# Threshold attention and SwiGLU feed-forward: 48 block loads of q and k move from SyncE's queue to GpSimd's own, the last group's output copies get buffers of their own, and the planner's ranks are set anew

## The chip, the cores and the metric

The kernel runs on one core of one Trainium2 chip. The metric is device time in microseconds (us) of one execution; the time before is the median of three runs. A profile of one execution, taken by the hardware profiler, goes with it. Its span, 532.7 us, is a little shorter than the device time of that run, 534.45 us. Five engines work beside each other: TensorE (PE in the profile, with its weight loads as PEld), VectorE (DVE), ScalarE (ACT), GpSimd (POOL) and SyncE (SP), the last used here only to issue DMAs. A queue name with a q (SPq, POOLq, ACTq) is an engine's instruction queue.

## What is computed

```python
batch, n_heads, seq, head_dim = (8, 8, 576, 64)        # q, k, v
scores = scale * np.matmul(q, k.transpose(0, 1, 3, 2))
thresh = np.max(scores, axis=-1, keepdims=True) - tau
scores = np.where(scores >= thresh, scores, -1000000000.0)
attn = softmax(scores)                                  # written out in the reference
attn_out = np.matmul(attn, v)
x = attn_out.transpose(0, 2, 1, 3).reshape(4608, 512)
xn = x / sqrt(mean(x * x) + 1e-6) * rms_g
g, val = xn @ w_gate, xn @ w_val                        # 512 -> 1536
out = (silu(g) * val) @ w_out                           # 1536 -> 512, float32
```

Only scores within `tau` (0.02) of the row's largest are kept, the rest is masked away before the softmax.

## The kernel before

**The work.** A batch has 576 rows: 512 "main" rows, cut into four chunks of 128, and 64 "tail" rows; the tails of two batches make one virtual chunk. That gives 36 chunks. A step is one chunk and one pair of heads, so there are 144 steps. One step runs so: TensorE writes the scores of two heads to PSUM (L697), VectorE copies them to a score buffer `ssb` with a running minimum of the negated scores (L730), GpSimd adds tau (`nth`, L771), ScalarE masks with a steep Prelu (L782, one per head) and takes the exponential to fp16 `wsb` (L789), a DMA transpose issued by SyncE turns it (`wt`, L849; the first 16 steps use TensorE instead), and every second step TensorE multiplies with v (L870, L875) and VectorE divides by the sums (L892, L893). After the four pairs of a chunk the rows are normalised (ScalarE L910, GpSimd L913 to L918), turned by one more DMA transpose (`xnT`, L922) and joined to groups of two or four chunks for the feed-forward part: gate and value matmuls (L976, L981), tanh on ScalarE (L990), two VectorE operations (L993, L998), the output matmuls (L1047, or L1022 in the last group), a copy out of PSUM that multiplies with 0.5 (L1060 on VectorE or L1062 on ScalarE) and a store (L1069, L1072, L1077). The feed-forward part of earlier chunks fills TensorE between the score bursts of later ones. At the end, from about 467 us on, only feed-forward work is left.

**Inputs.** Batches 0 and 1 take q and k through TensorE transposes. From batch 2 on (`BLOCKED = 2`) a batch's q and k come as 8 block loads, 288 KB each, 128 rows of 2304 contiguous bytes (`emit_block_loads`, L376): two pairs of heads for k, two for q, and the same again for the other half. So six batches make 48 loads, all issued by SyncE. They land in `qkx`. GpSimd then swaps 32x32 blocks in place through `spare` (L390, 24 copies a batch), and VectorE's 32x32 transposes (L403, L408, L412) turn the blocks into `qkt`, where the score matmuls read them. The buffer of a block is free again when VectorE's transposes of the batch before have read it. v is loaded by SyncE too (L609, L623) and rounded to fp16 by GpSimd (L584). The output weights are the only loads that GpSimd issues in the kernel before (L1138, four of 384 KB).

**Who sets the order.** Nothing is scheduled by hand line by line: `add` records each operation with an engine, a cost in ns, a priority (about the step it belongs to) and what it depends on. `order_ops` then plays a list scheduler: each engine takes, of those operations that could start first, the one with the lowest priority number, after `RANK` has been added to it by engine and kind. Loads marked `bulk` also hold back while more than 3.5 us of planned transfers are outstanding, and `gated` ties a load to the score burst of a given step. The result is a fixed sequence for each engine, and each engine runs its sequence in order: an instruction that waits holds up everything behind it on that engine. `LAT_QB` is the planned latency of a block load.

**The end.** The last group is "streamed": its four output tiles are accumulated in the four banks of the score tiles, and the last 4 of 12 slices of each tile are done tile after tile, in the order j = 0, 1, 2, 3. Tiles 0 and 2 are copied by VectorE, 1 and 3 by ScalarE. Tiles 0 and 1 go to the two output buffers `osb[0]`, `osb[1]`, which the group before has used as well, tiles 2 and 3 to score buffers, which are free by then. Each tile leaves in two stores of 64 rows.

## Time and profile before

| | before |
|---|---|
| device time, median of 3 runs | 534.09 us (533.53 to 534.13) |
| span of the profile | 532.7 us |
| mean granted TensorE clock | 0.999 |
| score bursts | from about 7 us to 467 us |
| feed-forward only | about 467 us to 527 us |
| GpSimd copies of L390, one | 0.66 us, 144 of them |
| DMA transposes of L849, issue on SyncE's queue | 1.32 us median, 128 of them |

The page of the profile gives, for each engine, the time in which it was busy, then the chain of work that ended last, followed back from the end, and the groups of instructions. A line of a group names the source line, the engine, the operation, what is written and what is read, shapes, and a count, then busy time, mean length and the idle time ahead. The timeline is in order of time: start, length (from the first start to the last end where several are merged), engine, line, operation, tiles, count, and in brackets the engine's idle time before it with what is thought to have ended it. That last part is inferred: a wait for several things is put down to the one that seems to have come last, and where a DMA was the last this can be wrong. In the table of waits each line is total us, number of times and the longest.

### The profile page before, as it was taken

Reading aid. Unit: us, or ns where it says so; the run is one execution under the profiler, and the core shown is the slowest. Engines: PE = TensorE matmul, PEld = TensorE weight load, DVE = VectorE, ACT = ScalarE, POOL = GpSimd, SP = SyncE. Lnnn points to the kernel's source line nnn. Section 1 sums busy time; section 2 is a strip of 40 time slices with the busy share of each in tenths; the row PEclk is TensorE's granted clock in tenths of the full one; section 3 lists DMA queues with packets and bytes.
Section 4 is the critical chain, followed back from the end, with each engine's and each line's share of the span. In section 5 each row is a group of like instructions: output and inputs, shape, how many; then the busy total and the mean of one; then the engine's idle time right before and its main releaser. Section 6 shows DMA issues by size and latency. Waiting matters only on the chain.

```text
span 532.7 us, 14403 instructions
## 1 busy us (share of the span) xinstructions
PE 521.8 (98%) x5368; PEld 275.2 (52%) x5368; DVE 465.3 (87%) x1347; ACT 444.0 (83%) x648; POOL 223.9 (42%) x478
## 2 busy tenths in 40 slices
PE   8999999999999999999999999999999999999995
PEld 4666676654555454545454544454545454454442
DVE  4899999979999899989997999999999898865641
ACT  5999999989997899889987998889998999952210
POOL 2368777424762165627733165626652111111000
PEclk9999999999999999999999999999999999999999
DMA  9999989979987888999989698998897677652003
GB/s 198 244 295 281 234 157 178 177 150 236 173 169 159 176 164 178 167 193 210 170 166 180 151 168 174 191 219 167 171 204 135 111 124 128 135 110 65 19 22 98
DMA packets 218886, 88.51 MB, mean 166 GB/s; under 512 B 195264, under 2 KB 204992, under 8 KB 218816
## 3 DMA queue, kind: packets, MB, share of 16 engines
q1 hardware_dynamic: 216016, 85.49, 80.9%
q0 software_dynamic: 1600, 1.57, 1.8%
q8 instruction: 42, 0.69, 0.5%
q10 hardware_dynamic: 1200, 0.52, 0.4%
q14 instruction: 28, 0.23, 0.1%
HBM read 37.75 MB, written 9.44 MB: 89 GB/s over the span
## 4 chain that ended last, share of the span: by engine, by line
PE 68%; DVE 12%; ACT 8%; DMA 4%; issue 3%; POOL 2%; SPq 1%; DVEq 0%; POOLq 0%; ACTq 0%
PE s_ps L697 21%; PE ring L1047 12%; PE ring L981 12%; PE ring L976 12%; DVE ssb L730 7%; ACT ssb L782 4%; PE ring L875 4%; DMA wt<-wsb 2%; PE s_ps L1022 2%; ACT wsb L789 2%; DMA qkx<-in_q_dram 2%; DVE sl L993 1%; PE ring L870 1%; ACT th L990 1%; PE s_ps L1047 1%
## 5 line engine op out<-in xcount | busy, mean ns | idle before, releaser
L782 ACT ACTIVATE ssb<-ssb,nth 128x576 f32<-128x576 f32 x288 | 209.2, 766 | 21.3 <-POOL nth L771 20.7
L730 DVE CUSTOM_DVE_ANT_0 ssb<-s_ps,zcol 128x576 f32<-128x576 f32 (+8 forms) x288 | 169.4, 634 | 6.2 <-PE s_ps L697 5.5
L697 PE MATMUL s_ps<-qkt 64*64 64x288 f32 (+8 forms) x2256 | 171.2, 411 | 1.2 <-DVE mx L730 0.8
L789 ACT ACTIVATE wsb<-ssb 128x1152 f16<-128x1152 f32 x144 | 166.7, 1158 | 2.2
L697 PEld LDWEIGHTS s_ps<-qkt 64*64 64x64 f32 x2256 | 81.9, 134 | 66.6 <-issue 28.0
L976 PE MATMUL ring<-xnT,wg 128*128 128x512 f16 (+1 forms) x464 | 109.2, 358 | 0.6 <-DVE sl L993 0.5
L981 PE MATMUL ring<-xnT,wv 128*128 128x512 f16 (+1 forms) x456 | 106.9, 357 | 0.5 <-DVE sl L993 0.2
L990 ACT ACTIVATE th<-ring 128x512 f32<-128x512 f32 (+1 forms) x116 | 62.5, 541 | 39.6 <-PE ring L976 39.2
L771 POOL TENSOR_SCALAR nth<-mx 128x2 f32<-128x2 f32 x144 | 30.8, 214 | 149.4 <-DVE mx L730 140.6
L993 DVE SCALAR_TENSOR_TENSOR sl<-th,ring 128x512 f32<-128x512 f32 (+1 forms) x116 | 71.9, 622 | 11.5 <-ACT th L990 11.2
L981 PEld LDWEIGHTS <-wv 128*128 128x128 f16 x480 | 44.6, 98 | 50.1 <-issue 10.8
L976 PEld LDWEIGHTS <-wg 128*128 128x128 f16 x480 | 43.0, 98 | 52.6 <-issue 15.1
L730 DVE CUSTOM_DVE_ANT_0 ssb<-s_ps,zcol,mxp 128x128 f32<-128x128 f32 (+7 forms) x112 | 52.8, 508 | 13.5 <-PE s_ps L697 13.3
L875 PE MATMUL ring<-va,wt 128*128 128x65 f16 (+1 forms) x1280 | 51.1, 193 | 0.0
L875 PEld LDWEIGHTS <-wt 128*128 128x128 f16 (+1 forms) x1280 | 46.1, 100 | 5.0 <-issue 0.6
L1047 PE MATMUL ring<-wo,hf 128*128 128x512 f16 x204 | 47.7, 379 | 0.0
L998 DVE TENSOR_TENSOR stg<-ring,sl 128x512 f16<-128x512 f32 (+1 forms) x57 | 35.5, 627 | 2.4
L998 DVE TENSOR_TENSOR hf<-ring,sl 128x512 f16<-128x512 f32 (+1 forms) x57 | 35.4, 626 | 1.8
L1047 PE MATMUL ring<-wo,stg 128*128 128x512 f16 x156 | 36.5, 379 | 0.0
L390 POOL COPY spare<-qkx 32x576 f32<-32x576 f32 x48 | 31.6, 658 | 8.7 <-DMA qkx<-in_k_dram 3.5
L893 DVE TENSOR_TENSOR xsb<-ring,rz 128x256 f32<-128x256 f32 x72 | 30.5, 424 | 3.5
L1047 PEld LDWEIGHTS <-hf 128*128 128x128 f16 x216 | 20.0, 98 | 25.8 <-issue 3.5
(75 smaller groups left out, 482.7 us busy)
## 6 DMA issues: line engine op xcount, KB each, us to landing
vst<-in_v_dram SPq DMA_DIRECT2D x32, 256.0 KB, 4.1
qkx<-in_k_dram SPq DMA_DIRECT2D x24, 288.0 KB, 3.5
qkx<-in_q_dram SPq DMA_DIRECT2D x24, 288.0 KB, 3.4
out_dram<-osb SPq DMA_DIRECT2D x51, 128.0 KB, 2.6
stg<-in_moe_w_gate_dram SPq DMA_DIRECT2D x6, 512.0 KB, 6.5
stg<-in_moe_w_val_dram SPq DMA_DIRECT2D x6, 512.0 KB, 6.4
wt<-wsb SPq DMA_TRANSPOSE x128, 3.6
out_dram<-osb SPq DMA_DIRECT2D x8, 256.0 KB, 3.0
```

The costliest lines, as they stand in the source:

```text
L390: nc.gpsimd.tensor_copy(out=dst, in_=at)
L697: nc.tensor.matmul(s_ps[h][rows, at:at + hi - lo], lhs(hs), k_of(bb, p, h)[hs, lo:hi], start=True, stop=True)
L730: nc.vector.tensor_tensor_reduce(out=ssb_of(s)[:, h, lo:hi], in0=s_ps[h][:, at:at + hi - lo], in1=zcol.to_broadcast([128, hi - lo]), scale ...
L782: nc.scalar.activation(out=sb_[:, h], in_=sb_[:, h], func=PRELU, scale=-1.0, bias=nth[m][:, h:h + 1], **PRELU_KW)
L789: nc.scalar.activation(out=wsb[s % NW], in_=sb_, func=AF.Exp)
L875: nc.tensor.matmul(ring[o.slot[0]][rs, at:at + D + 1], w[:, 5 * h + j, rs], va[vi][:, p, 2 * j + h], start=False, stop=(h == 1 and j == 3))
L976: nc.tensor.matmul(ring[o.slot[0]][:, 0:n], wg[d][:, fs], xnT[slot][:, d, 0:n], start=(d == 0), stop=(d == 3))
L981: nc.tensor.matmul(ring[o.slot[0]][:, 0:n], wv[d][:, fs], xnT[slot][:, d, 0:n], start=(d == 0), stop=(d == 3))
L990: nc.scalar.activation(out=th[i][:, 0:n], in_=ring[g.slot[0]][:, 0:n], func=AF.Tanh, scale=0.5)
L993: nc.vector.scalar_tensor_tensor(out=sl[i][:, 0:n], in0=th[i][:, 0:n], scalar=1.0, in1=ring[g.slot[0]][:, 0:n], op0=ALU.add, op1=ALU.mult)
L998: nc.vector.tensor_tensor(out=hf[hi][:, 0:n], in0=ring[vv.slot[0]][:, 0:n], in1=sl[i][:, 0:n], op=ALU.mult)
L1047: nc.tensor.matmul(ring[(first or o).slot[0]], hf[hs[fc][0]][:, 128 * j:128 * (j + 1)], wo[:, fc], start=(fc == 0), stop=(fc == NFC - 1))
```

## The change

Four edits. First, the 48 block loads of q and k are issued by GpSimd, and the planner is told so, with 880 ns of GpSimd's time each and a latency of 5.0 us in place of 4.0. Second, all four output tiles of the last group get parts of the score buffers, so that none of them shares a buffer with the group before. Third, the very last tile is copied in two halves of 256 columns, one by VectorE and one by ScalarE. Fourth, the planner's ranks are changed; kinds without an entry have rank 0. The first is for SyncE's queue, which carries all transposes, loads and stores in one order; the second and third are for the end; the fourth sets the order anew around the other three.

```diff
 RANK = dict(
-    ACT={"emit_ffn/ev": 450, "emit_ffn/store": 110, "emit_ffn/tanh": -300, "emit_k_tail/ev": -210, "emit_q_tail/ev": -80, "emit_qk/ev": 370,
-        "emit_softmax/ex2": 60, "emit_softmax/prelu": 220, "emit_x/sq": -330},
-    DVE={"emit_blocks/turn_k": 120, "emit_blocks/turn_kt": 288, "emit_blocks/turn_q": 293, "emit_burst/ttr": -57.4, "emit_ffn/ev": 320,
-        "emit_ffn/gate": 60, "emit_ffn/silu": -59, "emit_k_tail/ev": 80, "emit_qk/ev": -20, "emit_softmax/ev": 320, "emit_x/ev": 50},
-    PE={"emit_av/fn": -370, "emit_burst/fn": 16, "emit_ffn/gmm": 20, "emit_ffn/omm": 23, "emit_ffn/vmm": -40, "emit_k_tail/tr": 210, "emit_q_tail/tr":
-        -160, "emit_qk/tr": 60, "emit_softmax/tr": -40, "emit_x/trp": 20},
-    POOL={"emit_block_loads/swap": 40, "emit_softmax/nthr": -240, "emit_x/mean": -150, "emit_x/norm": -10, "round_/<lambda>": 130, "main/<lambda>":
-        700, "main/cast": -280},
+    ACT={"emit_ffn/ev": 440, "emit_ffn/store": 100, "emit_ffn/tanh": -280, "emit_k_tail/ev": -210, "emit_q_tail/ev": -60, "emit_qk/ev": 360,
+        "emit_softmax/ex2": 70, "emit_softmax/prelu": 250, "emit_x/sq": -300},
+    DVE={"emit_av/half": 10, "emit_blocks/turn_k": 120, "emit_blocks/turn_kt": 270, "emit_blocks/turn_q": 300, "emit_burst/ttr": -50,
+        "emit_ffn/ev_half": 20, "emit_ffn/silu": -47, "emit_k_tail/ev": 70, "emit_softmax/ev": 360, "emit_x/ev": 80},
+    PE={"emit_av/fn": -380, "emit_ffn/gmm": 20, "emit_ffn/omm": 22.5, "emit_ffn/vmm": -20, "emit_k_tail/tr": 220, "emit_q_tail/tr": -170,
+        "emit_qk/tr": 60, "emit_softmax/tr": -20, "emit_x/trp": 27.5},
+    POOL={"emit_block_loads/load": 10, "emit_block_loads/swap": 50, "emit_softmax/nthr": -250, "emit_x/mean": -140, "emit_x/norm": -20,
+        "round_/<lambda>": 120, "main/cast": -210},
 )
...
-    osb += [ssb[0][:, 0, 0:DM], ssb[0][:, 0, 0:DM], ssb[1][:, 0, 0:DM], ssb[2][:, 0, 0:DM]]
+    osb += [ssb[i % 3][:, i // 3, 0:DM] for i in range(4)]
...
-                    nc.sync.dma_start(out=own[:, a].rearrange("p r d -> p (r d)"),
+                    nc.gpsimd.dma_start(out=own[:, a].rearrange("p r d -> p (r d)"),
...
-                los.append(gated(add("SP", COST["sp_qb"], pr, before, load, dma=DMA_NS["qkb"] / GROUP, bulk=True), pr))
+                los.append(gated(add("POOL", COST["pool_dma"], pr, before, load, dma=DMA_NS["qkb"] / GROUP, bulk=True), pr))
...
-            oi = 2 + j if streamed and j > 1 else count["o"] % 2
+            oi = 2 + j if streamed else count["o"] % 2
...
+            final = streamed and j == len(parts) - 1
+
-            def ev(o, oi=oi, mo=mo, at=at, on_dve=on_dve):
+            def ev(o, oi=oi, mo=mo, at=at, on_dve=on_dve, cols=slice(DM // 2 if final else 0, DM)):
                 if on_dve:
-                    nc.vector.tensor_scalar(out=osb[oi], in0=ring[mo.slot[at]], scalar1=0.5, scalar2=None, op0=ALU.mult)
+                    nc.vector.tensor_scalar(out=osb[oi][:, cols], in0=ring[mo.slot[at]][:, cols], scalar1=0.5, scalar2=None, op0=ALU.mult)
                 else:
-                    nc.scalar.activation(out=osb[oi], in_=ring[mo.slot[at]], func=AF.Copy, scale=0.5)
+                    nc.scalar.activation(out=osb[oi][:, cols], in_=ring[mo.slot[at]][:, cols], func=AF.Copy, scale=0.5)
+
+            def ev_half(o, oi=oi, mo=mo, at=at):
+                cols = slice(0, DM // 2)
+                nc.vector.tensor_scalar(out=osb[oi][:, cols], in0=ring[mo.slot[at]][:, cols], scalar1=0.5, scalar2=None, op0=ALU.mult)
...
+            e = [e] + ([add("DVE", 340.0, pr - PUSH[0], [last_out[j]], ev_half)] if final else [])
...
-LAT_QB = 4000.0
+LAT_QB = 5000.0
```

More of the change, by code (lines that the diff above doesn't have):

```diff
@@ L1081, in emit_ffn @@
                     frees=(mo, at))
+            e = [e] + ([add("DVE", 340.0, pr - PUSH[0], [last_out[j]], ev_half)] if final else [])
             late = late and kind == "m"
-            osb_use[oi] = add("ACT" if late else "SP", (1100.0 if b >= BLOCKED else COST["sp"]) if kind == "m" else 1100.0, pr, [e], store,
+            osb_use[oi] = add("ACT" if late else "SP", (1100.0 if b >= BLOCKED else COST["sp"]) if kind == "m" else 1100.0, pr, e, store,
                               dma=DMA_NS['out'])
```

## The prediction

> **What bounds the kernel now.** I read the page first, engines and chain; then the table of waits; then the block loads in the list of DMA issues and on SyncE's queue; last the timeline of the end. Busy time by engine, and the chain by engine:
>
> ```profile
> PE 521.8 (98%) x5368; PEld 275.2 (52%) x5368; DVE 465.3 (87%) x1347; ACT 444.0 (83%) x648; POOL 223.9 (42%) x478
> PE 68%; DVE 12%; ACT 8%; DMA 4%; issue 3%; POOL 2%; SPq 1%; DVEq 0%; POOLq 0%; ACTq 0%
> ```
>
> TensorE is the bound: in nearly every 10 us stretch after 50 us it is busy 9.5 to 10 of 10, and the change gives it no matmul more or less. A gain can only come from a wait of TensorE that goes away, or from the few us after its last matmul. From 470 to 527 us nothing but feed-forward matmuls is left, 48 per 10 us, back to back.
>
> The table of waits says how much of TensorE's time hangs on the things that are moved:
>
> ```profile
> PE ring L870 <- DMA wt<-wsb: 1.0, 2, 0.8
> PEld L870 <- DMA wt<-wsb: 1.2, 2, 0.9
> ACT ssb L782 <- POOL nth L771: 20.7, 28, 2.2
> POOL spare L390 <- DMA qkx<-in_k_dram: 3.5, 3, 1.5
> ```
>
> TensorE waits 1.0 + 1.2 = 2.2 us in all for transposed weights that come through SyncE's queue. No engine but GpSimd waits for a block load, 3.5 us in three places, before swaps; VectorE's turns (L403, L408, L412) follow with no idle time ahead of them in any instance. So the loads are hidden now. The chain does give "DMA qkx<-in_q_dram" 1.7%, 3.89 us of it from 125.72 to 129.61. But the next link is ScalarE's Prelu at 129.63, which reads no q: it follows `nth`, which ran on GpSimd from 129.38 for 0.21 us. The load merely landed at the same moment, and I count that share as nothing.
>
> What one issue costs, on SyncE and on GpSimd (the second fence is the one line that GpSimd issues now, durations min/median/max in ns):
>
> ```profile
> qkx<-in_k_dram SPq DMA_DIRECT2D x24, 288.0 KB, 3.5
> qkx<-in_q_dram SPq DMA_DIRECT2D x24, 288.0 KB, 3.4
> wo<-in_moe_w_out_dram POOLq DMA_DIRECT2D x4, 384.0 KB, 7.9
> ```
>
> ```profile
> L1138 POOL DMA_DIRECT2D wo<-in_moe_w_out_dram x4: 828/857/990, 40.9 to 58.6; - x4
> ```
>
> SyncE's queue where loads and transposes meet:
>
> ```profile
> 121.82 0.45 SPq L376 DMA_DIRECT2D qkx<-in_q_dram  x1
> 122.38 3.29 SPq L849 DMA_TRANSPOSE wt<-wsb  x2
> 125.72 0.57 SPq L376 DMA_DIRECT2D qkx<-in_q_dram  x1
> 126.46 3.88 SPq L849 DMA_TRANSPOSE wt<-wsb  x2
> ```
>
> A load takes about 0.57 us of the queue, and here a transpose starts right after it, so it may have been held up by it. In the queue's timeline I count 13 of the 48 loads that have a transpose within 0.2 us behind them.
>
> The end:
>
> ```profile
> 522.77 0.69 DVE L1060 TENSOR_SCALAR osb<-ring 128x512 f32<-128x512 f32 x1 [4.79 <-PE ring L1047]
> 523.49 1.10 SPq L1077 DMA_DIRECT2D out_dram<-osb  x2
> 524.50 0.69 DVE L1060 TENSOR_SCALAR osb<-s_ps 128x512 f32<-128x512 f32 x1 [1.03 <-PE s_ps L1022]
> 526.30 0.69 DVE L1060 TENSOR_SCALAR ssb<-s_ps 128x512 f32<-128x512 f32 x1 [1.11 <-PE s_ps L1022]
> 527.02 1.10 SPq L1069 DMA_DIRECT2D out_dram<-ssb  x2
> 527.16 0.60 ACT L1062 ACTIVATE osb<-s_ps 128x512 f32<-128x512 f32 x1 [10.71 <-PE s_ps L1022]
> 527.66 0.59 ACT L1062 ACTIVATE ssb<-s_ps 128x512 f32<-128x512 f32 x1
> 528.86 0.59 SPq L1069 DMA_DIRECT2D out_dram<-ssb  x1
> ```
>
> Tile 2's copy starts at 526.30, so tile 1, which is done before it, was ready by about 525.4. Its copy (ScalarE, `osb`) starts only at 527.16. The line blames TensorE; I read it as the buffer: `osb[1]` was last stored from 523.49 to 524.59, and such stores land 2.6 us after issue by the page, at about 527.2.
>
> **What the Trainium skill says.** "DMA: Bandwidth & Descriptors", section "Issuing engines are not separate DMA queues": DMAs from any issuer run on the same 16 DMA engines and interleave; issuing from several saves only sequencer time. The trace cannot contradict it: the DMA share is already 0.8 to 1.2 in most 10 us stretches to 400 us, so I expect no bandwidth from the second queue. The same page, section "Latency and other measured facts", gives a first byte after about 1 us through GpSimd against 0.6 us, and the trace agrees in direction only (7.9 us against 3.5 us, but for 384 KB in the crowded first 60 us). "SBUF — State Buffer", section "SBUF: two separate sides", warns that GpSimd cannot write descriptors while VectorE runs a two-port operation. No run here shows such a stall: VectorE's steady work reads PSUM, and its turns take 0.75 us for 576 elements, a pace of one element at a time, so I price it at nothing.
>
> **The change, part by part.**
>
> Last group's buffers and the split copy. Tile 1 copies at about 525.4 and is stored by 526.9. The final tile's matmuls end about 0.86 us after tile 2's, at 527.15. Its halves take 0.38 us on ScalarE (a 128x256 tanh, L990) and 0.42 us on VectorE (128x256, L893), so both are done by about 527.6, against 528.25 now. SyncE has tile 2's two stores from 527.02 to 528.12, and then only the final one, at 528.17 instead of 528.86: 0.7 us earlier. The landing after it is as before. Gain 0.7 us; bounds 0.3 (a slower half-copy) and 1.0.
>
> 48 loads leave SyncE: 48 x 0.57 = 27 us of queue time, of which 13 x 0.57 = 7.4 us stood ahead of a transpose. What TensorE can get back is at most the 2.2 us it waits for `wt`; of the two longest transposes on the chain, at 285.02 and 340.93, neither has a load just ahead of it. I take 1.5 us, as freer stores and `xnT` transposes also shorten waits that the table puts elsewhere; bounds 0 and 2.5.
>
> 48 issues come to GpSimd: by L1138, 48 x 0.86 = 41 us, so 224 becomes 265 us, 50%. Bounds per issue 0.57 (SyncE's price for the same load) and 0.99. The new waits are on the load: for its gate, the score burst, and for VectorE's turns of the batch before. Queued behind it are `nth`, the normalisation (L913 to L918), the casts and the swaps. ScalarE's Prelu waits for `nth`; the swaps delay the turns, which have no wait to pass on. An `nth` comes every 460 / 144 = 3.2 us, so 0.86 / 3.2 = 27% of 48 issues, 13, meet one and delay it by 0.43 us on average: 5.6 us added to ScalarE's 20.7. TensorE's waits on what ScalarE makes are about a tenth of that 20.7 (the 2.2 us above), so 0.5 us reaches it; bounds 0 and 5.6.
>
> The landing later by a us or two, and `LAT_QB`: nothing, since the turns wait for no load. The ranks: they change every engine's order, and the profile does not price that. TensorE's weight loads wait 21.5 us in all for VectorE before score matmuls (mx 6.5, mxp 6.8, rz 4.4, xsb 3.8), so a better or worse interleaving can be worth some us either way; I take 0 for the point and 3 us either way for the range.
>
> Sum: -0.7 - 1.5 + 0.5 = -1.7 us, so 532.4.
>
> **Rivals.** *Nothing but the end*: the 2.2 us for `wt` are not caused by loads at all, as the two chain links suggest, and the ranks cancel: 534.1 - 0.7 = 533.4, no change that can be told. *GpSimd becomes the place where things queue*: in 50 to 60 us it is already busy 7.9 of 10, in 140 to 150 8.3, and a load that waits for its gate ahead of an `nth` holds ScalarE, itself busy 9.7 of 10 in most of these stretches; half of 5.6 us reaches TensorE, and the new order costs 1 us more: 534.1 - 0.7 + 2.8 + 1 = 537.2 at the hard end, typically 536, slower. For it speaks that ScalarE and VectorE are as full as TensorE, so slack is thin; against it that three score buffers give about 9.6 us for a loop of some 4.3 us (copies 1.4, `nth` 0.2, Prelu 1.4, exponential 1.2). *The order is the gain*: with SyncE's head of queue freer and FFN work ranked anew, TensorE loses a fifth less on 21.5 us (4.3): 534.1 - 1.7 - 4.3 + 1 = about 529.
>
> **How the numbers follow.** Small gain at 532.4: 0.38. Order gains at 529: 0.22. Nothing but the end: 0.17. GpSimd queues, slower: 0.23. Faster by over 0.2% (below 533.0) is the first two, 0.60; within 0.2% 0.17; slower 0.23. The range 528.5 to 537 leaves out about a tenth on each side: part of the order case and the hard end of the slower one.
>
> **What would show it.** Right: GpSimd busy near 265 us with L376 at about 0.86 us each; the last copies done near 0.5 us after TensorE's last matmul, and no ScalarE copy waiting 10 us; ScalarE's wait for `nth` up by at most 6 us; waits for block loads still only on GpSimd. Wrong: issues of well over 1 us, turns that wait for loads, `nth` waits up by more than 10 us, or score bursts that end more than 3 us away from 467 us, which would mean that the order and not the moved loads set the time.

## The result, and the profile after

| | before | after |
|---|---|---|
| device time, median of 4 runs each | 534.11 us (533.53 to 535.26) | 539.19 us (537.79 to 540.83) |
| span of the profile | 532.7 us | 539.0 us |
| last score matmul (L697) starts | 463.3 us | 468.4 us |
| last output matmuls (L1022) start | 522.57 us | 529.43 us |

The ratio after to before is 1.0094, with a 95% interval of 1.0066 to 1.0123: the change makes the kernel slower, by about 5 us. The prediction of 532.4 us was wrong, and its range ended at 537.0. The loss is there before the feed-forward part alone begins: the last score matmul starts 5.1 us later, and the part that was changed for the end is shorter than before.

The engines' busy times and the chain by engine, from the page of the kernel after:

```profile
PE 522.3 (97%) x5368; PEld 274.8 (51%) x5368; DVE 466.3 (87%) x1348; ACT 444.2 (82%) x648; POOL 252.1 (47%) x526
PE 67%; DMA 11%; DVE 11%; ACT 4%; issue 3%; POOL 2%; SPq 2%; POOLq 0%; DVEq 0%; ACTq 0%
```

TensorE has the same work, 522.3 us against 521.8, in a span that is 6.3 us longer. (The profiled execution after, 540.83 us, was the longest of its four, so the spans differ by more than the medians.) On the chain the DMA share has gone from 4% to 11%. The table of waits of the kernel after says which transfers:

```profile
ACT ssb L782 <- POOL nth L771: 21.4, 28, 3.4
PEld L870 <- DMA wt<-wsb: 6.9, 6, 2.6
ACT wsb L789 <- DMA wt<-wsb: 6.3, 4, 3.4
PE ring L870 <- DMA wt<-wsb: 5.8, 5, 2.5
DVE ssb L730 <- ACT wsb L789: 3.0, 2, 1.9
```

These are not waits for the loads that were moved. They are waits for `wt`, the transposed attention weights, which SyncE issues as before. TensorE's matmuls wait 5.8 us for them where they waited 1.0 us. The weight loads' 6.9 us are mostly the same moments seen a second time: in the timeline each waiting matmul of L870 stands within 0.01 us of a waiting weight load. New is that ScalarE waits too, 6.3 us: its exponential (L789) can't overwrite `wsb` before a transpose has read it. The wait for GpSimd's `nth`, which the prediction took for the main risk, is nearly as it was (20.7 before).

The DMA issues of the kernel after (last number: median us from issue to landing), then the `wt` transposes as a tile, first before and then after (issue time min/median/max in ns, first and last start; landing in us):

```profile
qkx<-in_k_dram POOLq DMA_DIRECT2D x24, 288.0 KB, 4.3
qkx<-in_q_dram POOLq DMA_DIRECT2D x24, 288.0 KB, 4.6
wt<-wsb SPq DMA_TRANSPOSE x128, 3.8
```

```profile
L849 SPq DMA_TRANSPOSE wt<-wsb x128: 1242/1316/2428, 61.2 to 473.4; - x128
DMA to landing us min/median/max: 3.2/3.6/6.2
```

```profile
L849 SPq DMA_TRANSPOSE wt<-wsb x128: 1255/1323/4747, 63.1 to 477.9; - x128
DMA to landing us min/median/max: 3.2/3.8/10.5
```

The median transpose is 0.2 us later, which nobody would notice. The worst is not: 10.5 us where it was 6.2, and one issue occupies SyncE's queue for 4.75 us where the longest was 2.43. That is a tail, and a table of medians hides it.

Where TensorE lost its time shows in the busy time by stretch of 10 us (start:end and length; then PE, PEld, DVE, ACT, POOL, each with its instruction count; granted clock, DMA share, GB/s). Before, then after:

```profile
70.00:80.00 10.00, 9.82 (x128) 7.22 (x126) 8.90 (x27) 9.97 (x19) 6.71 (x13) 1.00 0.90 170
130.00:140.00 10.00, 10.00 (x124) 5.23 (x123) 9.93 (x32) 9.27 (x15) 6.85 (x14) 1.00 1.03 188
```

```profile
70.00:80.00 10.00, 7.67 (x97) 5.35 (x94) 7.23 (x22) 8.22 (x15) 6.70 (x13) 1.00 1.16 190
130.00:140.00 10.00, 7.49 (x82) 3.42 (x75) 7.96 (x22) 6.28 (x10) 4.58 (x8) 1.00 1.22 234
```

In these two stretches alone TensorE is busy 4.7 us less than before (9.82 - 7.67 + 10.00 - 7.49), at full clock. The timeline of the second one, of the kernel after:

```profile
121.75 0.64 POOL L376 DMA_DIRECT2D qkx<-in_k_dram  x1
...
122.75 0.58 POOL L376 DMA_DIRECT2D qkx<-in_k_dram  x1
...
123.12 2.24 SPq L849 DMA_TRANSPOSE wt<-wsb  x1
...
124.09 1.10 POOL L376 DMA_DIRECT2D qkx<-in_q_dram  x2
...
126.81 14.01 SPq L849 DMA_TRANSPOSE wt<-wsb  x4
...
133.75 1.16 ACT L789 ACTIVATE wsb<-ssb 128x1152 f16<-128x1152 f32 x1 [3.45 <-DMA wt<-wsb]
...
134.94 0.69 DVE L730 CUSTOM_DVE_ANT_0 ssb<-s_ps,zcol 128x512 f32<-128x512 f32 x1 [1.89 <-ACT wsb L789]
...
136.96 0.23 PE L870 MATMUL ring<-va,wt 128*128 128x130 f16 x1 [2.51 <-DMA wt<-wsb]
```

GpSimd issues four loads, 4 x 288 KB, within 3.4 us. The transpose issued at 123.12, in their midst, lands after 10.54 us, the next (126.81) after 10.11, and the one at 131.66 after 9.40 (times of single issues in the trace). From there it spreads in a ring: ScalarE can't write the next `wsb`, VectorE has no score buffer (1.89 us), TensorE no `wt` (2.51 us). In the kernel before, SyncE's queue had transposes and loads in turn in this phase, as the prediction showed, and the transposes issued from 122.38 to 126.46 landed after 3.9 to 4.9 us.

The order of transfers alone doesn't explain this stretch. Two of the four loads took 9.2 and 9.6 us themselves and landed at 133.31 and 134.22 us, about when the first of these transposes did (133.67). The DMA engines were busy and yet moved little (columns as above; after, then before):

```profile
126.00:132.00 6.00, 6.00 (x58) 2.65 (x53) 5.49 (x18) 4.13 (x6) 2.95 (x6) 1.00 1.19 121
126.00:132.00 6.00, 6.00 (x75) 2.71 (x66) 5.86 (x15) 5.79 (x9) 2.54 (x6) 1.00 1.26 211
```

From 126 to 132 us they moved 121 GB/s, where the kernel before moved 211; from 68 to 74 us, ahead of the loss in the first of the two stretches, the kernel after moved 94. TensorE's two long waits for `wt` end at 75.01 and at 136.96, behind these two stretches, and are 2.33 + 2.51 = 4.8 of its 5.8 us. So where most of the time was lost, the DMA engines as a whole were slow. What made them slow is not shown by any run; the program with two queues by themselves, further down, has a case without this and one with it.

The end of the kernel after:

```profile
531.36 0.69 DVE L1062 TENSOR_SCALAR ssb<-s_ps 128x512 f32<-128x512 f32 x1 [1.03 <-PE s_ps L1022]
...
532.23 0.60 ACT L1064 ACTIVATE ssb<-s_ps 128x512 f32<-128x512 f32 x1 [8.04 <-PE s_ps L1022]
...
533.17 0.69 DVE L1062 TENSOR_SCALAR ssb<-s_ps 128x512 f32<-128x512 f32 x1 [1.11 <-PE s_ps L1022]
534.10 0.42 DVE L1068 TENSOR_SCALAR ssb<-s_ps 128x256 f32<-128x256 f32 x1 [0.24 <-PE s_ps L1022]
534.56 0.38 ACT L1064 ACTIVATE ssb<-s_ps 128x256 f32<-128x256 f32 x1 [1.74 <-DVE ssb L1068]
534.98 0.47 ACTq L1075 DMA_DIRECT2D out_dram<-ssb  x1
```

Tile 1 is now copied in its turn, at 532.23, between tiles 0 and 2; before, it came after tile 2. But the two halves of the last tile are not done beside each other: ScalarE's half starts when VectorE's has ended, and the bracket names VectorE as what it waited for. From the start of the last L1022 matmuls to the end of the trace it is 9.61 us, against 10.11 before: the end gains 0.5 us.

A reading of my own, worked out from issue and landing of each transfer in the trace: the 128 `wt` transposes, sorted by how many of the 48 block loads were in flight at some time between their issue and their landing (number of transposes, mean landing):

```
loads in flight       0           1           2           3           4 or more     all
before            66, 3.79    22, 3.78    28, 3.77    12, 4.47    none          3.85 us
after             60, 3.73    23, 3.99    27, 4.26    12, 5.42    6, 8.40       4.27 us
```

With no load beside it a transpose takes the same time in both kernels. On one queue the number of loads matters little: even in the run with the ranks alone, below, three transposes on SyncE's queue have four loads beside them and take 4.28 us. With the loads on a second queue it matters, and four are in flight more often. A late transpose also meets more loads just by being late; but counted at the moment of its issue the difference stays: with two loads in flight then, a transpose takes 4.19 us before (9 of them) and 5.80 after (17). This became the theory to test.

### The profile page after: what moved, and what is told of

Its sections match the earlier page's. It is cut to its first block, busy times and chain, and to the rows that moved or that the text cites. A ratio compares the mean times of both kernels' runs of the same rounds, so it can differ in the third digit from the quotient of the medians.

```text
span 539.0 us, 14400 instructions
## 1 busy us (share of the span) xinstructions
PE 522.3 (97%) x5368; PEld 274.8 (51%) x5368; DVE 466.3 (87%) x1348; ACT 444.2 (82%) x648; POOL 252.1 (47%) x526
## 4 chain that ended last, share of the span: by engine, by line
PE 67%; DMA 11%; DVE 11%; ACT 4%; issue 3%; POOL 2%; SPq 2%; POOLq 0%; DVEq 0%; ACTq 0%
PE s_ps L697 19%; PE ring L976 12%; PE ring L981 12%; PE ring L1047 12%; DMA wt<-wsb 7%; DVE ssb L730 6%; PE ring L875 4%; PE s_ps L1022 2%; ACT ssb L782 2%; PE ring L870 2%; DVE sl L993 1%; ACT wsb L789 1%; DMA stg<-in_moe_w_val_dram 1%; DMA qkx<-in_k_dram 1%; PE s_ps L1047 1%
## 5 line engine op out<-in xcount | busy, mean ns | idle before, releaser
L730 DVE CUSTOM_DVE_ANT_0 ssb<-s_ps,zcol 128x576 f32<-128x576 f32 (+8 forms) x288 | 169.3, 635 | 10.4 <-PE s_ps L697 6.0
L789 ACT ACTIVATE wsb<-ssb 128x1152 f16<-128x1152 f32 x144 | 166.7, 1158 | 8.4 <-DMA wt<-wsb 6.3
L697 PE MATMUL s_ps<-qkt 64*64 64x288 f32 (+8 forms) x2256 | 171.2, 411 | 1.2 <-DVE mx L730 0.8
L697 PEld LDWEIGHTS s_ps<-qkt 64*64 64x64 f32 x2256 | 81.7, 134 | 67.0 <-issue 27.2
L981 PE MATMUL ring<-xnT,wv 128*128 128x512 f16 (+1 forms) x460 | 108.0, 357 | 0.1
L870 PE MATMUL ring<-va,wt 128*128 128x130 f16 (+1 forms) x160 | 32.2, 224 | 5.8 <-DMA wt<-wsb 5.8
L390 POOL COPY qkx<-spare 32x576 f32<-32x576 f32 x48 | 31.8, 663 | 3.0
```

Source lines behind the costliest of these rows:

```text
L697: nc.tensor.matmul(s_ps[h][rows, at:at + hi - lo], lhs(hs), k_of(bb, p, h)[hs, lo:hi], start=True, stop=True)
L730: nc.vector.tensor_tensor_reduce(out=ssb_of(s)[:, h, lo:hi], in0=s_ps[h][:, at:at + hi - lo], in1=zcol.to_broadcast([128, hi - lo]), scale ...
L789: nc.scalar.activation(out=wsb[s % NW], in_=sb_, func=AF.Exp)
L870: nc.tensor.matmul(ring[o.slot[0]][rs, at:at + 2 * (D + 1)], w[:, 4, rs], va[vi][:, p, 8:10].rearrange("p e d -> p (e d)"), start=True, st ...
L981: nc.tensor.matmul(ring[o.slot[0]][:, 0:n], wv[d][:, fs], xnT[slot][:, d, 0:n], start=(d == 0), stop=(d == 3))
```

## The experiments

Theory A: the loads on a queue of their own overtake the transposes on SyncE's queue, transposes land up to 7 us late, and the ring of `wsb`, `ssb` and `wt` stalls. Rival B: GpSimd's time, 28 us of issues ahead of `nth` and swaps. Rival C: the new ranks. Rival D: something else in issuing a load from GpSimd, whatever its bytes. In what follows a difference in us against the kernel before is (ratio - 1) x 534.1, from the ratio to the runs of the kernel before that were measured beside it.

### The queue alone

```diff
-                    nc.sync.dma_start(out=own[:, a].rearrange("p r d -> p (r d)"),
+                    nc.gpsimd.dma_start(out=own[:, a].rearrange("p r d -> p (r d)"),
```

In the kernel before; its plan still takes the load for SyncE's.

> The kernel before, with one word changed: the 48 block loads are issued by GpSimd at the same places of the old plan; the orders of TensorE, VectorE and ScalarE stay as before, and so do ranks and the end. If the second queue itself makes the loss (block loads in flight beside the transposes delay these), about 538 to 540 us, and transposes that land 8 to 10 us after issue. If the new order of work makes the loss, 533 to 535 us with transposes landing as before (median 3.6, at most 6.2 us). If GpSimd's time makes it, more waiting of ScalarE for nth than 25 us.

Measured 543.22 us (540.01 to 546.27), ratio 1.0154 (1.0118 to 1.0190): 8.2 us slower, more than the whole change and more than any of the three cases expected. Its slowest transpose lands after 8.1 us, at the low end of the 8 to 10. From its table of waits:

```profile
ACT ssb L782 <- POOL nth L771: 28.7, 36, 2.5
POOL spare L390 <- DMA qkx<-in_k_dram: 9.4, 7, 2.0
PE ring L870 <- DMA wt<-wsb: 2.8, 7, 0.6
```

The moved queue is enough to make a loss. But here it comes by two ways: `wt` later (2.8 against 1.0), and GpSimd's sequence, which was not planned for it. Swaps wait 9.4 us for loads that land later (3.5 before), with `nth` behind them, and ScalarE waits 8 us more for `nth`. So waits on GpSimd are real where the plan doesn't know of the loads; in the changed kernel, which plans for them, `nth` rose by 0.7 us only.

### The change with the loads back on SyncE

The same line of the changed kernel back to `nc.sync`. All compute engines keep the sequence of the changed kernel, so ranks, `LAT_QB` and end are as there; a load only changes the engine that issues it.

> The changed kernel, with one word changed: the block loads are issued by SyncE again, at the places of the new plan; all compute orders are those of the changed kernel. If the queue makes the loss, 532 to 535 us. If the new order makes it, 538 to 540 us. In between if both have a part.

Measured 533.63 us (532.36 to 535.36), ratio 0.9978 (0.9970 to 0.9987): 1.2 us faster than before. The chain by engine:

```profile
PE 86%; DVE 7%; POOL 2%; DMA 2%; issue 1%; ACT 1%; SPq 0%; DVEq 0%; POOLq 0%
```

No wait for `wt` is in its table of waits, and DMA is 2% of the chain. One word takes away the whole loss and more: 1.0094 - 0.9978 = 1.16%, 6.2 us, hang on which queue carries the loads (the ends of the two intervals put it between 4.2 and 8.2). Rival C falls: the new sequence, with the end that comes with it, is a little better than the old.

### The end alone, and the ranks alone

The kernel before with the edits of the end only (buffers, split copy), and with the new `RANK` only:

```diff
-    osb += [ssb[0][:, 0, 0:DM], ssb[0][:, 0, 0:DM], ssb[1][:, 0, 0:DM], ssb[2][:, 0, 0:DM]]
+    osb += [ssb[i % 3][:, i // 3, 0:DM] for i in range(4)]
...
-            oi = 2 + j if streamed and j > 1 else count["o"] % 2
+            oi = 2 + j if streamed else count["o"] % 2
...
+            e = [e] + ([add("DVE", 340.0, pr - PUSH[0], [last_out[j]], ev_half)] if final else [])
```

> The kernel before with the edits of the end alone (own buffers for the last four tiles, last tile copied in two halves); loads on SyncE, old ranks. Predicted gain of these edits 0.7 us, so 533.4; from the changed kernel's trace, in which the two halves run one after the other and the end from the last group of matmuls is 0.56 us shorter, 533.5. If the end is bound elsewhere, 534.1.

Measured 534.11 us (532.59 to 536.02), ratio 0.9991 (0.9981 to 1.0000): 0.5 us, which agrees with the trace, though the interval reaches to no gain at all.

> The kernel before with the new ranks alone; loads planned and issued on SyncE, old end. If the new order of work is the loss, 538 to 540 us; if the queue is, 532 to 535 us.

Measured 536.78 us (536.11 to 538.54), ratio 1.0042 (1.0029 to 1.0056): 2.2 us slower, between the two cases expected. Its table of waits has

```profile
POOL spare L390 <- DMA qkx<-in_k_dram: 5.8, 2, 3.1
```

(3.5 before). The ranks alone cost 2.2 us, and the same ranks with the end, `LAT_QB` and loads planned on GpSimd, but issued by SyncE, gain 1.2 us. So an order's worth isn't a sum over its numbers. Perhaps the ranks fit a plan in which SyncE isn't taken up by loads; which part of that plan helps was not tried.

### GpSimd's time alone

The loads on SyncE, and in the place of each load's issue three small operations on GpSimd:

```diff
+                    for _ in range(3):
+                        nc.gpsimd.tensor_scalar(out=busy, in0=busy, scalar1=1.0, scalar2=None, op0=ALU.mult)
-                    nc.gpsimd.dma_start(out=own[:, a].rearrange("p r d -> p (r d)"),
+                    nc.sync.dma_start(out=own[:, a].rearrange("p r d -> p (r d)"),
```

> Loads issued by SyncE at the places of the new plan (as in the 533.6 us kernel), and at each load's place GpSimd does three small operations on a scratch tile, about 0.6 us, as long as its issue of a load took. If GpSimd's time is what the moved loads cost, 537 to 540 us; if it is hidden, 533 to 534.5 us and ScalarE's wait for nth stays near 20 us.

Measured 532.84 us (532.10 to 534.91), ratio 0.9980 (0.9972 to 0.9989), the same as without them (0.9978). The engines of its page:

```profile
PE 520.6 (98%) x5368; PEld 274.8 (52%) x5368; DVE 465.3 (88%) x1349; ACT 443.8 (84%) x648; POOL 254.9 (48%) x622
```

GpSimd is busy 254.9 us, more than the 252.1 of the change, and it costs nothing. These operations don't wait for anything, as a load might; but in the changed kernel the table of waits has 0.2 us of idle time ahead of L376 in all. Rival B falls for the changed kernel.

### The loads spread out on GpSimd

In the changed kernel, each load moved later in GpSimd's sequence until the planned starts lie 2.5 us apart:

```diff
+    at = -1e9
+    for o in [x for x in seq if x.bulk and "emit_block_loads" in x.fn.__qualname__]:
+        at = max(o.start, at + 2500.0)
+        i = seq.index(o)
+        seq.remove(o)
+        while i < len(seq) and seq[i].start < at and o not in seq[i].deps:
+            i += 1
+        seq.insert(i, o)
```

> The changed kernel, loads still issued by GpSimd on its own queue, but each load moved later in GpSimd's sequence until at least 2.5 us of planned time lie between one load and the next; nothing else moves. If two and more block loads in flight at once beside the transposes make the loss, most of it goes: 534 to 536 us, transposes that take over 5 us to land fall from 23 to about 12, and TensorE's wait for wt from 12.7 to under 5 us. If a load on a second queue hurts whatever the pace, or GpSimd's issue does, 538 to 540 us stay.

Measured 544.1 us (537.57 to 549.38), ratio 1.0136 (1.0095 to 1.0178). The expectation was wrong by some 8 us: this is no cure but the worst of the variants built on the changed kernel. Its `wt` tile and its waits:

```profile
DMA to landing us min/median/max: 3.2/3.9/12.9
```

```profile
PEld L870 <- DMA wt<-wsb: 9.9, 8, 5.1
ACT wsb L789 <- DMA wt<-wsb: 9.7, 6, 3.3
PE ring L870 <- DMA wt<-wsb: 8.5, 7, 5.0
```

Planned distances were not kept on the chip: five transposes still had four or more loads beside them, and took 10.93 us on average (12.88 at worst). In the worst stretch three loads issued between 121.4 and 126.6 us took 9 us each to land, together with two stores on SyncE's queue. Like the changed kernel's worst stretch, this one slowed loads, stores and transposes alike. So this run doesn't tell what a true spacing does; it only shows once more that the loss goes with late transposes. And "four at once" isn't the whole of it, since two or three loads already gave 5.0 and 5.5 us, against 4.3 and 5.4 in the changed kernel.

### The loads on ScalarE's queue

```diff
-                    nc.gpsimd.dma_start(out=own[:, a].rearrange("p r d -> p (r d)"),
+                    nc.scalar.dma_start(out=own[:, a].rearrange("p r d -> p (r d)"),
```

> The changed kernel, loads issued by ScalarE at the same places of the plan, so on a second queue[...]. 48 x 0.6 = 29 us of ScalarE's time come on top, so the time says little by itself (536 to 545). What tells is the landing of the transposes that have two and more loads in flight beside them: if any second queue hurts them, 4.3 us and more as with GpSimd (4.26, 5.42, 8.40 for 2, 3, 4 loads); if only GpSimd's descriptors do, 3.8 to 4.4 us as on the common queue.

Measured 536.74 us (535.23 to 537.79), ratio 1.0046 (1.0030 to 1.0061): 2.5 us slower than before, 3.6 us slower than the loads on SyncE (1.0046 - 0.9978). The `wt` transposes took 4.54, 5.12 and 6.90 us with two, three and four loads beside them. So late transposes don't need GpSimd: a second queue on another engine makes them too, with a loss a little over half as large. ScalarE pays 0.335 us per issue besides, 16 us in all on an engine that is 83% busy, so not all 3.6 us need be the transposes. The profile doesn't settle it: it is of the shortest execution (535.23 us), in which TensorE waits 0.7 us for `wt`.

### Half of the loads

```diff
-                    nc.gpsimd.dma_start(out=own[:, a].rearrange("p r d -> p (r d)"),
+                    (nc.gpsimd if src is k else nc.sync).dma_start(out=own[:, a].rearrange("p r d -> p (r d)"),
```

> The changed kernel, with the 24 loads of k issued by GpSimd and the 24 of q by SyncE, at the same places of the plan. If the loss grows with what is in flight on the second queue beside transposes, it lies between 533.6 us (none there) and 539.2 (all there), nearer to the first since at most two loads then pile up: 534 to 536.5. If any use of the second queue costs the whole, 538 to 540.

Measured 535.2 us (533.74 to 538.19), ratio 1.0010 (0.9992 to 1.0028). With 0, 24 and 48 loads on GpSimd the ratio is 0.9978, 1.0010 and 1.0094, and TensorE's matmuls wait for `wt` less than the table shows, 1.6 and 5.8 us. By the middle values the loss grows faster than the number of loads; the intervals would still allow a straight line.

### Two queues by themselves

A program that leaves out the attention and the feed-forward part altogether: eight transposes of a 128x1152 fp16 tile by SyncE and eight block loads of k, alone and together, with a wait for everything between the stages. It ran once.

```diff
+    def both(eng):
+        for i in range(N):
+            load(eng, i)
+            turn(i)
+    stages = [turns, lambda: loads(nc.sync), lambda: loads(nc.gpsimd), lambda: loads(nc.scalar),
+              lambda: both(nc.sync), lambda: both(nc.gpsimd), lambda: both(nc.scalar)]
```

> Not the kernel's work: a program of DMAs alone, without any of the attention or feed-forward computation (its stores carry no result). Seven stages, each begun when the stage before has landed, the seven run twice: 8 transposes of 128x1152 fp16 (as L849) from SyncE; 8 block loads of 288 KB (as L376) from SyncE; 8 from GpSimd; 8 from ScalarE; then 8 loads and 8 transposes together, both from SyncE in turn; loads from GpSimd, transposes from SyncE; loads from ScalarE, transposes from SyncE. If loads and transposes from two queues slow each other in the DMA engines, a transpose packet of 256 bytes takes over twice as long in the sixth stage as in the fifth, single transposes land after 6 us and more, and the sixth stage is longer than the transposes alone by more than the loads' own time (about 6 to 8 us). If two queues share the engines without loss, the sixth stage is shorter than the fifth, near the longer of the two alone (about 13 us), and packets take as long as in the fifth.

From issue and landing in its trace (first issue to last landing, first pass and second; landings of the eight transposes in the first pass):

```
stage                              first, second      transposes' landings, us
transposes alone                   13.39, 13.69       3.4 3.4 3.4 3.4 3.5 3.5 3.4 3.3
loads alone: SyncE                  9.03,  9.99
             GpSimd                 9.37,  9.59
             ScalarE                9.32,  9.63
both on SyncE, in turn             19.74, 19.39       3.6 3.8 4.1 3.8 4.9 4.7 4.1 4.0
loads GpSimd, transposes SyncE     19.46, 20.47       5.6 10.4 8.8 3.4 3.6 3.6 3.4 3.4
loads ScalarE, transposes SyncE    24.37, 23.83       6.4 12.2 12.6 9.0 6.7 6.3 5.2 3.4
```

The theory as I had put it failed in part: with GpSimd's queue the stage isn't longer, and a transpose's packet (a record of 256 B in the trace) takes no longer, 21 ns alone, 21 and 23 ns beside the loads. Nor is the stage shorter, as sharing without loss would have it. What changes is the order of service. In its timeline, VectorE reads each result when it has landed; the first stretch is both on SyncE, the second the loads on GpSimd:

```profile
49.79 0.15 DVE L63 CAST acc<-turned 128x1 f32<-128x1 f16 x1 [3.92 <-DMA turned<-src]
...
52.03 0.15 DVE L63 CAST acc<-turned 128x1 f32<-128x1 f16 x1 [1.99 <-DMA turned<-src]
...
54.34 0.15 DVE L63 CAST acc<-turned 128x1 f32<-128x1 f16 x1 [2.08 <-DMA turned<-src]
...
71.79 0.15 DVE L63 CAST acc<-turned 128x1 f32<-128x1 f16 x1 [5.70 <-DMA turned<-src]
...
77.83 0.15 DVE L63 CAST acc<-turned 128x1 f32<-128x1 f16 x1 [5.78 <-DMA turned<-src]
...
78.80 0.15 DVE L63 CAST acc<-turned 128x1 f32<-128x1 f16 x1 [0.74 <-DMA turned<-src]
```

On one queue a transpose comes every 2 us or so. On two, the first comes after 5.7 us, the second 6 us later, when all eight loads have landed, and then the rest as fast as without loads. From 71 to 76 us the DMA engines move 351 GB/s, so nothing is slow here; the bytes are the loads'. The Trainium skill offers a reason, on the page "DMA: Bandwidth & Descriptors" under "Queues, rings and completion order": a DMA engine takes turns between the queues it has work for, and changes over only after a whole packet. Pieces of unequal size would then share the time unequally. The trace agrees with this in the mean only: in the six 1 us bins from 70 to 76 us, 430 records of 4608 B of the loads pass beside 487 of 256 B of the transposes, about one to one (the page counts larger packets than these records, so only the ratio is meant). But bin by bin it goes from 0.4 to 2 records of a transpose for one of a load, and from 69 to 70 us it is 916 to 4. So the turns are a likely reading, not a shown one. With transposes alone some 800 of their records pass in 1 us.

With ScalarE's queue the two together also lose throughput, 24 us in place of 19.5: from 90 to 100 us the DMA engines move 172 GB/s. This is nearer to the changed kernel's bad stretches (121 and 94 GB/s) than the stage with GpSimd's queue. Why is open.

### Fewer bytes, same queue

The changed kernel with the same 48 issues on GpSimd, each of which brings 64 of the 576 columns of its rows (the other columns of q and k from batch 2 on aren't loaded); and the same thin loads on SyncE as a control. Two fills of parts of `qkx` at the start are in both.

```diff
-                    nc.gpsimd.dma_start(out=own[:, a].rearrange("p r d -> p (r d)"),
-                                      in_=src[b, 2 * p:2 * p + 2].rearrange("h (m r) d -> h m (r d)", r=RUN))
+                    nc.gpsimd.dma_start(out=own[:, a, 0],
+                                      in_=src[b, 2 * p:2 * p + 2].rearrange("h (m r) d -> h m (r d)", r=RUN)[:, :, 0:D])
```

> The changed kernel, but each of the 48 loads on GpSimd's queue brings only the first 64 of the 576 columns of its 128 rows (32 KB in place of 288 KB); the other columns keep what lay there, so most of q and k from batch 2 on is not loaded. Same instructions, same queue, same plan. If the loss is made by bytes of a second queue that overtake the transposes (theory), nothing is left to overtake: time within 1 us of the same thin loads on SyncE, 531 to 534 us, no transpose with a landing over 7 us, TensorE's waits for transposed weights under 2 us in all. If it is made by something else in issuing from GpSimd, its semaphores, its descriptors or the order of the plan (rival), the bytes do not matter: 4 us or more above the same loads on SyncE, 537 to 539 us.

> The same thin loads (first 64 of 576 columns, the rest of q and k from batch 2 on not loaded), issued by SyncE: the control for the thin loads on GpSimd. Both theories: 531 to 534 us, at or a little under the kernel with whole loads on SyncE (533.6), since TensorE hardly waited for a transpose there.

Measured 535.77 us (534.05 to 536.55) on GpSimd, ratio 1.0017 (1.0006 to 1.0029), and 534.02 us (533.16 to 534.91) on SyncE, ratio 0.9984 (0.9972 to 0.9996). The `wt` transposes of the first, and the only lines of its table of waits in which TensorE waits for them (this kernel's lines stand two further down, so L872 is L870 elsewhere):

```profile
DMA to landing us min/median/max: 3.2/3.4/6.3
```

```profile
PEld L872 <- DMA wt<-wsb: 0.4, 1, 0.4
PE ring L872 <- DMA wt<-wsb: 0.3, 1, 0.3
```

With one ninth of the bytes the late transposes are gone (6.3 us at most, 10.5 with whole loads; 3.75 us on average beside two thin loads), and the price of GpSimd's queue falls from 6.2 us to 1.0017 - 0.9984 = 0.33%, 1.8 us. Neither theory gets it whole: A wanted within 1 us, D 4 us or more. So some 4.4 of the 6.2 us hang on the bytes of the loads, and 1.8 us (0.5 to 3.0 by the ends of the intervals) remain even without them. Fewer bytes are also fewer and smaller records, on GpSimd's queue 16 of 2048 B to a load in place of 64 of 4608 B, which these runs don't tell apart; nor do they tell whether the bytes act by passing the transposes or by slowing everything. The 1.8 us aren't in TensorE's wait for `wt`, since the control has the same two lines. The profiled execution of the thin GpSimd kernel was its shortest (534.05 us), so its trace doesn't show where they go; that stays open.

### A version that beats both

The changed kernel with the loads on SyncE, and the last tile copied whole by ScalarE:

```diff
-                    nc.gpsimd.dma_start(out=own[:, a].rearrange("p r d -> p (r d)"),
+                    nc.sync.dma_start(out=own[:, a].rearrange("p r d -> p (r d)"),
...
-            final = streamed and j == len(parts) - 1
+            final = False
```

> Loads issued by SyncE at the places of the new plan, and the last tile copied whole by ScalarE instead of in two halves, which the trace shows one after the other (0.42 us, then 0.38 us, with a wait between). If that wait is all, the last copy ends about 0.3 us earlier: 533.3 against 533.6 us. If the halves gave anything, 533.6 or more.

Measured 532.73 us (532.19 to 533.77), ratio 0.9971 (0.9958 to 0.9984): the lowest here, 1.5 us better than before. The end, from its timeline:

```profile
525.17 0.69 DVE L1062 TENSOR_SCALAR ssb<-s_ps 128x512 f32<-128x512 f32 x1 [1.11 <-PE s_ps L1022]
526.03 0.60 ACT L1064 ACTIVATE ssb<-s_ps 128x512 f32<-128x512 f32 x1 [1.21 <-PE s_ps L1022]
526.66 0.49 ACTq L1075 DMA_DIRECT2D out_dram<-ssb  x1
```

The whole copy ends 526.63 - 525.17 = 1.46 us after tile 2's copy starts; the two halves in the changed kernel end 534.94 - 533.17 = 1.77 us after it. So the last copy is done 0.3 us sooner, as expected, but the program isn't: from the start of the last L1022 matmuls to the end it is 9.62 us here, and 9.61 to 9.63 in the changed kernel and in the two runs above that have the split (loads back on SyncE, end alone). With and without it SyncE issues the very last store 5.8 us after that start, right behind tile 2's two stores, and it lands at 8.7 us. So the split neither costs nor gains anything, and the gain of the end comes from the buffers. The times don't say otherwise: with the split and without it the intervals overlap (0.9970 to 0.9987 and 0.9958 to 0.9984).

## Why the prediction was wrong

Step by step, as it put them:

- **TensorE is the bound, and the loads are hidden.** Right for both kernels: TensorE has 522 us of work, and no waits for a load of q or k took the time. But "hidden" was read as "free to move". What mattered was whom the loads disturb, not who waits for them.
- **End, -0.7 us.** The mechanism was right for the buffers: tile 1 is copied in its turn. The size was off, 0.5 us in the trace and in the run with the end alone. The term that was mis-sized is the last store on SyncE's queue. It was to move from 6.29 to 5.60 us after the start of the last L1022 matmuls and came at 5.83, since tile 2's two stores ahead of it took 1.25 us and not 1.10. That the two halves of the copy ran one after the other (0.42 + 0.38 us), and not side by side, was a second error, but without effect: they were done at 5.51.
- **48 loads leave SyncE, -1.5 us.** It didn't come. TensorE's wait for `wt` went up from 1.0 to 5.8 us. The bound of 2.2 us was also too high by itself, since it added TensorE's 1.0 us and the weight loads' 1.2 us, which are the same two moments (290.5 and 346.0 us of the kernel before). More than 1.0 us of direct wait was not there to be gained.
- **48 issues on GpSimd, +0.5 us.** Too high on every count, without harm: an issue takes 0.59 us and not 0.86 (next fence), GpSimd went to 252 us and not 265, the wait for `nth` rose by 0.7 us and not by 5.6. The row of 0.86 us was for a load of another shape and 384 KB; the lower bound, SyncE's 0.57 for the same load, was the better neighbour. The step from 5.6 to 0.5 us took TensorE's 2.2 us as a wait on what ScalarE makes; it is a wait for `wt`. The run with GpSimd's time alone puts the whole term at nothing. Of GpSimd's issues held up by VectorE, which the prediction priced at nothing, there is no sign: none takes more than 0.66 us.
- **The landing later, nothing.** This is the step that failed. It looked at the landing of the loads alone, found that nobody waits for it (true: they land at 4.3 and 4.6 us, from 3.5 and 3.4, and it cost nothing), and took "no bandwidth from the second queue" to mean no effect on anything else. What it didn't price is the landing of everything that stays on SyncE's queue while loads are in flight on another. In the kernel after, that is 3.7 us for a transpose with no load beside it and 8.4 beside four, and TensorE, ScalarE and VectorE wait for it in a ring. The loads on GpSimd's queue cost 6.2 us against the same loads on SyncE's, of which some 4.4 go when they bring a ninth of the bytes; 1.8 stay unexplained. How the loads make the transposes late, by passing them or by slowing all transfers, the runs leave open.
- **Ranks, 0 with 3 us either way.** Within its bounds: 2.2 us slower alone, and with the rest of the plan part of a gain of 1.2 us.
- **What would show it.** One sign of being wrong came: the score bursts end later, by 5.1 us. But it was to mean that the order and not the moved loads set the time, and that is refuted: with the same order and the loads on SyncE the last score matmul starts at 461.3 us, earlier than before (463.3).

GpSimd's issues in the kernel after, as lines of one tile (issue time in ns, min/median/max):

```profile
L376 POOL DMA_DIRECT2D qkx<-in_k_dram x24: 538/597/658, 61.6 to 375.9; - x24
L376 POOL DMA_DIRECT2D qkx<-in_q_dram x24: 538/576/647, 62.8 to 381.4; - x24
```

In sum: -1.2 us for plan and end with the loads on SyncE's queue, +6.2 us for the second queue, together +5.0 us. (The 6.2 us are the difference of two measured kernels, so this sum must come out.) Of the rivals, the one on the slower side had the right sign and the wrong cause: it had GpSimd's queue holding back `nth`, which happened only with the queue moved and the plan left alone.

Could it have been seen? The prediction rested on the section "Issuing engines are not separate DMA queues" of the Trainium skill's page "DMA: Bandwidth & Descriptors", which says that the issuers share the same DMA engines and that several issuers save only sequencer time. In these runs they also cost 6.2 us. The turns between queues, on the same page under "Queues, rings and completion order", and two facts of the profile of before could have raised the question: the DMA share was about 1 in many stretches, so what goes first can make something else wait; and SyncE's queue, by its order, let no load or one through between two transposes, seldom two, and three once. So its order spaced the loads out among the transposes, and its removal was priced as a relief only.

What stays open: the 1.8 us of thin loads; and the two stretches of the changed kernel behind which TensorE loses most of its time, as from 126 to 132 us, in which the records of the loads take about 440 to 680 ns each, against 180 to 240 elsewhere in that phase. The program with two queues by themselves, with GpSimd, doesn't show that. So it is shown that the queue makes the loss and that most of it hangs on the loads' bytes; the way from there to the late transposes is in part argued.

## What to carry to other kernels

Before a transfer that nobody waits for moves to another queue, ask which transfers it will then be able to pass or to slow: on one queue the order of issue keeps the bulk and the urgent transfers in turn, on two it does not. Here the DMA share was near 1 and a short transfer (a transpose of 256 B pieces) was on the path of the bound engine; keeping the bulk in the same queue, or making it smaller, took away all or most of the loss. Look at the longest landing, not at the median, and at the bytes moved in the stretch where it falls.

## What the runs showed that I had not expected

- With loads on GpSimd's queue, total time for eight loads and eight transposes is that of one queue (19.46 and 20.47 us against 19.74 and 19.39), but single transposes land after 10.4 and 11.5 us in place of 3.6 to 4.9.
- With loads on ScalarE's queue the same work takes 24.37 and 23.83 us: two queues cost throughput there. In the changed kernel most of TensorE's lost time follows two stretches in which the DMA engines moved only 121 and 94 GB/s.
- The last tile's copy, done 0.3 us sooner, didn't end the program sooner, since the last store waited for its place in SyncE's queue.
- A load's records in the trace are 4608 B on GpSimd's queue and 2304 B on SyncE's and ScalarE's, for the same 288 KB.
- The six runs with the loads spread out on GpSimd's queue lie between 537.57 and 549.38 us, the 22 of the changed kernel with its loads on SyncE's between 532.36 and 535.36.
